# Attention into two mixture layers on one core: maxima of the keys as a tree, the opening in another order, weight splits and routing steps in other places

## The chip, the cores and the metric

The kernel runs on one core of a Trainium2 chip. The metric is the device time of one execution in microseconds (us). Line numbers (L298) are lines of the kernel before.

## The reference

Three stages follow one another, all in fp32. The attention has 8 batches, 8 heads, 576 positions and 64 features; a softmax over the features is taken of the queries and a softmax over the positions of the keys, so that each head needs only a 64x64 product of keys and values.

```python
q_s = exp(q - max(q, -1));  q_s /= sum(q_s, -1) + 1e-9        # over 64 features
k_s = exp(k - max(k, seq)); k_s /= sum(k_s, seq) + 1e-9       # over 576 positions
kv  = einsum('bhsd,bhse->bhde', k_s, v)
x   = einsum('bhsd,bhde->bhse', q_s, kv).transpose(0, 2, 1, 3).reshape(4608, 512)
h   = x @ w_in                                                # 512 -> 2048
x   = (h * clip(h + 3, 0, 6) / 6) @ w_out                     # 2048 -> 512
e   = argmax(x @ w_gate, 1)                                   # one of 8 experts for each token
out = softmax(x @ w_gate)[e] * sigmoid(x @ w_output_gate)[e] * (relu(x @ w1[e]) @ w2[e])
```

The weights `w_in` and `w_out` arrive as 64-bit floats and are turned into fp32 on the chip.

## The kernel before

*Tiling.* The first part (attention, the dense layers and the choice of the expert) goes over 16 groups of 288 tokens (96 partitions by 3), two groups to a batch. A group takes 16 steps, one for each 128 of the 2048 hidden columns (`fb`). A step of group `g` issues, in this order: `h_mm` (L390, the product with `w_in`), `h_ev` (activation on Scalar at L398, product on Vector at L399, from group 1 on a cast on Scalar at L405 and a subtraction on GpSimd at L406), `tail` (the last copies of the group before), the attention work of the *next* group that `att_steps` assigns to this step, `x2_mm` of the step three earlier (L417, the product with `w_out`), and last a routing step of the group *before*: `route1` at step 4, `route2` at 6, `route3` at 9, `route4` at 11. The second part, over the routed tokens, starts when all 16 groups are through.

*Order.* All this is written out by hand. Each engine takes its instructions in the order in which they are written, and an instruction that waits holds up what is behind it on its engine. A step's order in the code is so also the order on TensorE, Scalar, Vector and GpSimd.

*Splits.* Group 0 multiplies in plain fp32 with whole weights. From group 1 on each operand is a sum of two fp32r parts, high and low, and a product is three matmuls for each 128 of the depth: 12 for `h_mm` and 12 for `x2_mm` in a step. `split` makes the two parts of a weight: a cast on Scalar (L200), then a subtraction (L202), on Vector for "in" (`w_in`) and on GpSimd for "out" (`w_out`). It takes a slot of the pool `wsl` (33 slots) for the pair and gives the slot of the raw weight back behind the subtraction. Group 0 decodes the raw weights (`dec_act` on Scalar, `dec_vec` on Vector) and splits "in" 0 at step 5 and "in" 1 and 2 at steps 14 and 15. Group 1 splits at each step the "in" weight that is used three steps later, and the "out" weight of that step.

*Attention.* The keys of a batch are worked on in four head pairs during the odd group before the batch (groups 1, 3, ... 13) and, for the first batch, in the opening. For each pair: `k_max` (maximum over six rows of a partition, L275), `k_max_tr` (transposed on TensorE), `k_max_diag` (maximum over partitions, and a diagonal matrix `dg` of it, L292), `k_max_row` (`kmrow`, L298, which spreads the maximum over all partitions), `k_sub` (L306), `k_exp` (L311), `kv_mm` (L319), and `kv_ev` (L326 to L330, division by the sum, into `kvbd`). For each group: `q_a`, `q_exp`, `q_b`, then `q_tr` (transposed queries `qtps`, copied to `qT` at L363) and `x0_mm` (L376) four times each. The copies of the result to `xhi` (L377) and `xlo` (L379) are what the next group's `h_mm` reads.

*Routing.* `route2` transposes the logits (`ltps`, L460), copies and adds them (L462, L463) and picks the expert. `route3` counts tokens by two small matmuls (`rkps`) and goes on at L490 to L494.

*PSUM.* Eight banks: two for `h_mm` (pool `ph`), four for `x2_mm` (pool `pacc`), and two (pool `pat`) for everything else: `kmps`, `kmrow`, `kvps`, `qtps`, `x0ps`, `lgps`, `ltps` and `rkps` take these in turn.

*Opening.* Before group 0 the first batch's keys and queries are worked on one after the other, and `pe_warm` issues matmuls (L220) whose result nobody reads. `load_k`, `load_q`, `load_v` and `load_w_raw` are issued ahead of all.

Of the kernel before, what the change touches and what calls it, by code (L numbers as in the profile page):

```python
# [8 lines left out]
F32 = mybir.dt.float32  # L9
# [6 lines left out]
ALU = mybir.AluOpType  # L16
AX = mybir.AxisListType
# [3 lines left out]
def kernel(  # L21
# [13 lines left out]
    nc = tc.nc  # L35
    B, H, S, D = q.shape
# [4 lines left out]
    PR = S // R  # L41
# [83 lines left out]
    def big(shape, dt, tag, bufs, name):  # L125
        return sb.tile(shape, dt, tag=tag, name=name, bufs=bufs)
# [145 lines left out]
    def k_max(b, hp):  # L272
        t = kt[b, hp]
        m = sb.tile([PR, 2, D], F32, tag="km", name="km", bufs=2)
        nc.vector.tensor_reduce(out=m, in_=t.rearrange("p r h d -> p h d r"), axis=AX.X, op=ALU.max)  # L275
        kmp[b, hp] = m

    def k_max_tr(b, *hps):
# [62 lines left out]
    def q_exp(g, a):  # L341
        t = qt[g, a].rearrange("p r h d -> p (r h d)")
        nc.scalar.activation(out=t, in_=t, func=ACTF.Exp)
# [520 lines left out]
    with tc.manual_schedule():  # L864
# [17 lines left out]
        pe_warm(10)  # L882
        k_max(0, 0)
        k_max_tr(0, 0)
        q_a(0, 0)
        q_exp(0, 0)
        k_max_diag(0, 0)
        k_max_row(0, 0)
        k_max(0, 1)
        k_max_tr(0, 1)  # L890
        k_sub(0, 0)
        k_exp(0, 0)
        v_pad(0, 0)
        k_max_diag(0, 1)
        k_max_row(0, 1)
        q_b(0, 0)
        k_max(0, 2)
        k_sub(0, 1)
        k_max_tr(0, 2)
        k_exp(0, 1)  # L900
        v_pad(0, 1)
        kv_mm(0, 0)
        k_max_diag(0, 2)
        k_max_row(0, 2)
        kv_ev(0, 0)
        q_a(0, 1)
        k_max(0, 3)
        k_sub(0, 2)
        q_tr(0, 0)
        k_max_tr(0, 3)  # L910
        kv_mm(0, 1)
        k_exp(0, 2)
        v_pad(0, 2)
        q_exp(0, 1)
        k_max_diag(0, 3)
        k_max_row(0, 3)
        kv_ev(0, 1)
        k_sub(0, 3)
        x0_mm(0, 0)
        q_tr(0, 1)  # L920
        k_exp(0, 3)
        v_pad(0, 3)
        kv_mm(0, 2)
        q_b(0, 1)
        dec_act(0)
        x0_mm(0, 1)
        kv_ev(0, 2)
        dec_vec(0)
        kv_mm(0, 3)
        q_tr(0, 2)  # L930
        dec_act(1)
        kv_ev(0, 3)
        dec_vec(1)
        x0_mm(0, 2)
        q_tr(0, 3)
        x0_mm(0, 3)
        dec_act(2)
        dec_act(3)
        for g in range(NG):
            st = att_steps(g + 1)  # L940
            for fb in range(NF):
                h_mm(g, fb)
                if g == 0:
                    load_w_raw(2)
                    decode_step(fb + 1)
                    if fb in (5, NF - 2, NF - 1):
                        split("in", max(0, fb - NF + 3))
                    if fb == 14:
                        gate_weights()
                if g == 0 and fb == 13:  # L950
                    clear_table()
                if g > 0 and fb == 2:
                    logits(g - 1, 0)
                    x2_ev(g - 1, 3)
                h_ev(g, fb)
                if g == 1:
                    if fb + 3 < NF:
                        split("in", fb + 3)
                if g > 0:
                    tail(g - 1, fb)  # L960
                if g == 1:
                    if fb < NF - 1:
                        split("out", fb)
                    if fb == 3:
                        split("out", NF - 1)
                for f in st[fb]:
                    f()
                if fb >= 3:
                    x2_mm(g, fb - 3)
                if fb == NF - 1:  # L970
                    x2_mm(g, fb - 2)
                if g > 0:
                    if fb == 4:
                        route1(g - 1)
                    if fb == 6:
                        route2(g - 1)
                    if fb == 9:
                        route3(g - 1)
                    if fb == 11:
                        route4(g - 1)  # L980
                if g == NG - 2 and fb == 11:
                    plan_first(g - 1)
                if g == NG - 1:
                    if fb == 1:
                        b_tab(0)
                    if fb == 2:
                        b_tab(1)
                    if fb == 3:
                        b_idx(0)
                    if 4 <= fb < 8:  # L990
                        b_gather(0, 2 * fb - 8)
                        b_gather(0, 2 * fb - 7)
                    if fb == 5:
                        for c in range(4):
                            b_load(0, c)
                    if 10 <= fb < 14:
                        b_x(0, fb - 10)
                    if fb >= 7 and fb < 15:
                        for c in (2 * fb - 14, 2 * fb - 13):
                            b_split(0, c)  # L1000
                            if c + 4 < NCH:
                                b_load(0, c + 4)
# [134 lines left out]
```

## Time and profile before

| | us |
|---|---|
| median of 3 runs | 1475.05 (1471.15 to 1476.66) |
| the profiled execution | 1475.42 |
| its span in the profile | 1473.7 |
| TensorE busy in the span | 1405.4 |
| VectorE busy | 868.1 |
| ScalarE busy | 677.7 |
| GpSimd busy | 480.8 |
| opening, before the first matmul of group 0 | 33.87 |
| group 0 | 65.38 |
| group 1 | 84.61 |
| group 2, an even one | 55.61 |
| group 3, an odd one | 64.35 |

The mean granted clock of TensorE over the span is 0.989 of full speed. The times of the groups are distances between the first matmuls of `h_mm` in the trace. In the profile PE is TensorE (matmuls), PEld its weight loads, DVE is VectorE, ACT is ScalarE, POOL is GpSimd. `out<-in` are the program's names for the tiles. A bracket at the end of a row, as in `[0.92 <-DVE w L202]`, says how long the engine stood idle before the instruction and which one ended that.

The views in the section on rows have these columns. *Stretches*: the stretch and its length, then busy time and number of instructions of PE, PEld, DVE, ACT and POOL, then the granted clock of TensorE (1.00 is 2.4 GHz, the upper of two levels, 1.2 GHz is the lower), the busy share of the DMA engines, and GB/s. *Waits*: who waits for whom, then total us, number of waits, the longest. *Timeline*: start and length in us, engine, line, operation, tiles and shapes, number of instructions of one kind in a row. *Groups by line and form*: the number of instructions, their busy time and the mean ns of one, then the idle time of the engine ahead of them.

### The profile page before, as it was taken

What the parts mean: (1) busy time and instruction counts of PE and PEld (TensorE: products, weight loads), DVE (VectorE), ACT (ScalarE), POOL (GpSimd) and SP (SyncE); (2) the same over time, 40 slices, a digit from 0 to 9 for tenths busy, and PEclk for the clock granted to TensorE, in tenths of its full rate; (3) what the DMA queues carried; (4) which work ended last, traced back from release to release, by engine and by line L of the source; (5) the groups of instructions that cost most, each with busy time, mean ns of one, the idle gap of its engine ahead of it and who ended that gap; (6) DMA issues with size and microseconds to landing.
All of it is one profiled execution on the core that took longest, in us unless ns stands there. A gap on an engine that the chain in (4) does not pass through costs nothing. (4 is left out here: it accounts for less than half of the span.)

```text
span 1473.7 us, 27644 instructions
## 1 busy us (share of the span) xinstructions
PE 1405.4 (95%) x9728; PEld 1319.8 (90%) x9728; DVE 868.1 (59%) x2164; ACT 677.7 (46%) x1494; POOL 480.8 (33%) x546
## 2 busy tenths in 40 slices
PE   6997799999999999999999999999999899999997
PEld 5776799999999999999999999999878788888886
DVE  6976454544734635545454473647878476766743
ACT  5855433433433433343343343345555465555642
POOL 1114423222223222222322222245454544445431
PEclk7999999999999999999999999999999999999998
DMA  9912021220221202212122020034767676777773
GB/s 308 306 31 50 17 57 25 49 49 17 58 52 23 49 17 57 48 27 57 25 49 49 18 57 17 2 103 144 239 200 229 187 234 212 246 222 232 232 257 122
DMA packets 195750, 161.19 MB, mean 109 GB/s; under 512 B 116828, under 2 KB 147793, under 8 KB 195602
## 3 DMA queue, kind: packets, MB, share of 16 engines
q1 hardware_dynamic: 186114, 139.51, 32.7%
q0 software_dynamic: 9488, 19.82, 4.3%
q8 instruction: 79, 1.29, 0.4%
q14 instruction: 69, 0.57, 0.1%
HBM read 139.03 MB, written 20.49 MB: 108 GB/s over the span
## 5 line engine op out<-in xcount | busy, mean ns | idle before, releaser
L417 PE MATMUL acc<-gh,w 128*128 128x288 f32 x1920 | 437.6, 305 | 0.0
L390 PE MATMUL hps<-xhi,w 128*128 128x288 f32 x1920 | 425.2, 297 | 0.0
L406 POOL TENSOR_TENSOR gl<-r,gh 128x288 fp32r<-128x288 f32 x240 | 194.2, 811 | 600.0 <-ACT gh L405 556.2
L417 PEld LDWEIGHTS acc<-gh,w 128*128 128x128 f32 x1920 | 321.1, 189 | 3.5
L390 PEld LDWEIGHTS hps<-xhi,w 128*128 128x128 f32 x1920 | 321.4, 188 | 0.9
L399 DVE SCALAR_TENSOR_TENSOR r<-r,hps 128x288 f32<-128x288 f32 x240 | 108.2, 451 | 316.2 <-ACT r L398 308.4
L390 PE MATMUL hps<-xlo,w 128*128 128x288 f32 x960 | 283.2, 295 | 0.0
L417 PE MATMUL acc<-gl,w 128*128 128x288 f32 x960 | 283.0, 295 | 0.0
L398 ACT ACTIVATE r<-hps,half 128x288 f32<-128x288 f32 x240 | 120.1, 500 | 278.6 <-PE hps L390 275.4
L817 PE MATMUL h2ps<-x2h,wb 128*128 128x256 f32 x1088 | 217.3, 282 | 6.4 <-DVE hl L822 4.5
L771 POOL DMA_INDIRECT gx<-x2d,idx x148 | 162.0, 1094 | 145.9 <-issue 132.3
L736 DVE TENSOR_TENSOR wb<-rawb,wb 128x512 fp32r<-128x512 f32 x296 | 191.8, 688 | 14.0 <-ACT wb L735 5.5
L817 PEld LDWEIGHTS h2ps<-x2h,wb 128*128 128x128 f32 x1088 | 176.2, 188 | 16.0 <-DVE hl L822 8.2
L835 PE MATMUL y<-wb,hh 128*128 128x512 f32 x592 | 189.1, 401 | 1.4 <-issue 1.4
L417 PEld LDWEIGHTS acc<-gl,w 128*128 128x128 f32 x960 | 181.7, 189 | 3.0
L390 PEld LDWEIGHTS hps<-xlo,w 128*128 128x128 f32 x960 | 180.9, 188 | 0.2
L405 ACT CAST gh<-r 128x288 fp32r<-128x288 f32 x240 | 103.9, 433 | 152.8 <-DVE r L399 152.3
L735 ACT CAST wb<-rawb 128x512 fp32r<-128x512 f32 x296 | 167.9, 618 | 0.0
L817 PE MATMUL h2ps<-x2l,wb 128*128 128x256 f32 x544 | 152.8, 281 | 3.8 <-DVE x2l L801 3.0
L821 ACT ACTIVATE hh<-h2ps 128x256 fp32r<-128x256 f32 (+1 forms) x160 | 59.0, 369 | 180.3 <-PE h2ps L817 93.4
L822 DVE SCALAR_TENSOR_TENSOR hl<-h2ps,hh 128x256 fp32r<-128x256 f32 (+1 forms) x160 | 63.4, 396 | 126.9 <-ACT hh L821 70.0
L835 PE MATMUL y<-wb,hl 128*128 128x512 f32 x296 | 117.3, 396 | 1.7 <-issue 1.7
(201 smaller groups left out, 1730.6 us busy)
## 6 DMA issues: line engine op xcount, KB each, us to landing
rawb<-in_moe_w_dram SPq DMA_DIRECT2D x296, 256.0 KB
x2d<-xrow SPq DMA_DIRECT2D x60, 144.0 KB
raw<-in_moe_w_in_dram SPq DMA_DIRECT2D x16, 512.0 KB
raw<-in_moe_w_out_dram SPq DMA_DIRECT2D x16, 512.0 KB
qt<-in_q_dram SPq DMA_DIRECT2D x112, 72.0 KB
kt<-in_k_dram SPq DMA_DIRECT2D x56, 144.0 KB
vt<-in_v_dram SPq DMA_DIRECT2D x56, 144.0 KB
w1h<-in_moe_w_dram SPq DMA_DIRECT2D x24, 256.0 KB
```

Of the source, the lines that this page charges most:

```text
L390: nc.tensor.matmul(ps[:, 0:G], weight("in", fb, part, kk), x[:, kk, :], start=(n == 0), stop=(n == len(parts) * KD - 1))
L398: nc.scalar.activation(out=r, in_=ps[:, 0:G], func=ACTF.Relu, bias=half, scale=1.0 / 6.0)
L399: nc.vector.scalar_tensor_tensor(out=r, in0=r, scalar=1.0, in1=ps[:, 0:G], op0=ALU.min, op1=ALU.mult)
L405: nc.scalar.copy(gh, r)
L406: nc.gpsimd.tensor_tensor(out=gl, in0=r, in1=gh.bitcast(F32), op=ALU.subtract)
L417: nc.tensor.matmul(acc[g][eb][:, 0:G], weight("out", fb, part, eb), x, start=(fb == 0 and n == 0), stop=(fb == NF - 1 and n == len(parts) ...
L735: nc.scalar.copy(w[:, 0, :], raw)
L736: nc.vector.tensor_tensor(out=w[:, 1, :], in0=raw, in1=w[:, 0, :].bitcast(F32), op=ALU.subtract)
L771: nc.gpsimd.indirect_dma_start(out=st["gx"][:, kk, :], out_offset=None, in_=x2q, in_offset=bass.IndirectOffsetOnAxis(ap=st["idx"][:, kk:kk ...
L817: nc.tensor.matmul(ps[:, 0:m], w[:, wl, c], x[:, kk, 0:m], start=(kk == 0 and n == 0), stop=(kk == KD - 1 and n == 2))
L822: nc.vector.scalar_tensor_tensor(out=hl[:, 0:m], in0=ps[:, 0:m], scalar=0.0, in1=hh[:, 0:m].bitcast(F32), op0=ALU.max, op1=ALU.subtract)
L835: nc.tensor.matmul(st["y"][t2], hx[:, c], w[:, wl, :], start=(fb == 0 and n == 0), stop=(fb == NF2 - 1 and n == 2))
```

## The change

The maximum over six rows of the keys is taken by three operations of two inputs each (384, 128 and 128 elements for a partition) instead of one reduction; the result of the first is a scratch tile in the slots of `xs`. In the opening the steps of the four head pairs are interleaved otherwise, pairs 2 and 3 share the operations that follow their maxima, `q_a` stands further back, and three more `pe_warm` of 4 matmuls each are written between the steps. Of the "in" splits, 0 to 6 are now made in group 0 (at steps 5 and 12 to 15) instead of 0 to 2; group 1 makes the other nine, seven steps ahead of their use instead of three, and issues both its splits ahead of `h_ev` instead of behind it. `route2` and `route3` are issued behind `h_ev`, ahead of `tail` and of the step's attention work, instead of at the end of the step.

```diff
--- before.py
+++ after.py
@@ -272,7 +272,10 @@
     def k_max(b, hp):
         t = kt[b, hp]
         m = sb.tile([PR, 2, D], F32, tag="km", name="km", bufs=2)
-        nc.vector.tensor_reduce(out=m, in_=t.rearrange("p r h d -> p h d r"), axis=AX.X, op=ALU.max)
+        m3 = big([PR, 3, 2, D], F32, "xs", 3, "km3")
+        nc.vector.tensor_tensor(out=m3, in0=t[:, 0:3], in1=t[:, 3:6], op=ALU.max)
+        nc.vector.tensor_tensor(out=m, in0=m3[:, 0], in1=m3[:, 1], op=ALU.max)
+        nc.vector.tensor_tensor(out=m, in0=m, in1=m3[:, 2], op=ALU.max)
         kmp[b, hp] = m
 
     def k_max_tr(b, *hps):
@@ -882,57 +885,57 @@
         pe_warm(10)
         k_max(0, 0)
         k_max_tr(0, 0)
-        q_a(0, 0)
-        q_exp(0, 0)
+        pe_warm(4)
+        k_max(0, 1)
         k_max_diag(0, 0)
         k_max_row(0, 0)
-        k_max(0, 1)
         k_max_tr(0, 1)
+        pe_warm(4)
         k_sub(0, 0)
         k_exp(0, 0)
         v_pad(0, 0)
         k_max_diag(0, 1)
         k_max_row(0, 1)
-        q_b(0, 0)
-        k_max(0, 2)
+        pe_warm(4)
+        q_a(0, 0)
+        q_exp(0, 0)
         k_sub(0, 1)
-        k_max_tr(0, 2)
         k_exp(0, 1)
         v_pad(0, 1)
         kv_mm(0, 0)
-        k_max_diag(0, 2)
-        k_max_row(0, 2)
+        k_max(0, 2)
+        k_max(0, 3)
+        k_max_tr(0, 2, 3)
+        kv_mm(0, 1)
+        q_b(0, 0)
+        k_max_diag(0, 2, 3)
+        k_max_row(0, 2, 3)
         kv_ev(0, 0)
-        q_a(0, 1)
-        k_max(0, 3)
         k_sub(0, 2)
-        q_tr(0, 0)
-        k_max_tr(0, 3)
-        kv_mm(0, 1)
         k_exp(0, 2)
         v_pad(0, 2)
+        q_tr(0, 0)
+        kv_ev(0, 1)
+        q_a(0, 1)
         q_exp(0, 1)
-        k_max_diag(0, 3)
-        k_max_row(0, 3)
-        kv_ev(0, 1)
         k_sub(0, 3)
-        x0_mm(0, 0)
-        q_tr(0, 1)
         k_exp(0, 3)
         v_pad(0, 3)
         kv_mm(0, 2)
+        x0_mm(0, 0)
+        q_tr(0, 1)
         q_b(0, 1)
+        kv_ev(0, 2)
+        kv_mm(0, 3)
+        x0_mm(0, 1)
         dec_act(0)
-        x0_mm(0, 1)
-        kv_ev(0, 2)
+        q_tr(0, 2)
+        kv_ev(0, 3)
         dec_vec(0)
-        kv_mm(0, 3)
-        q_tr(0, 2)
-        dec_act(1)
-        kv_ev(0, 3)
-        dec_vec(1)
         x0_mm(0, 2)
         q_tr(0, 3)
+        dec_act(1)
+        dec_vec(1)
         x0_mm(0, 3)
         dec_act(2)
         dec_act(3)
@@ -943,8 +946,8 @@
                 if g == 0:
                     load_w_raw(2)
                     decode_step(fb + 1)
-                    if fb in (5, NF - 2, NF - 1):
-                        split("in", max(0, fb - NF + 3))
+                    for f in {5: (0,), 12: (1,), 13: (2,), 14: (3, 4), 15: (5, 6)}.get(fb, ()):
+                        split("in", f)
                     if fb == 14:
                         gate_weights()
                 if g == 0 and fb == 13:
@@ -952,17 +955,20 @@
                 if g > 0 and fb == 2:
                     logits(g - 1, 0)
                     x2_ev(g - 1, 3)
-                h_ev(g, fb)
                 if g == 1:
-                    if fb + 3 < NF:
-                        split("in", fb + 3)
-                if g > 0:
-                    tail(g - 1, fb)
-                if g == 1:
+                    if fb + 7 < NF:
+                        split("in", fb + 7)
                     if fb < NF - 1:
                         split("out", fb)
                     if fb == 3:
                         split("out", NF - 1)
+                h_ev(g, fb)
+                if g > 0 and fb == 6:
+                    route2(g - 1)
+                if g > 0 and fb == 9:
+                    route3(g - 1)
+                if g > 0:
+                    tail(g - 1, fb)
                 for f in st[fb]:
                     f()
                 if fb >= 3:
@@ -972,10 +978,6 @@
                 if g > 0:
                     if fb == 4:
                         route1(g - 1)
-                    if fb == 6:
-                        route2(g - 1)
-                    if fb == 9:
-                        route3(g - 1)
                     if fb == 11:
                         route4(g - 1)
                 if g == NG - 2 and fb == 11:
```

## Rows read from the trace of the kernel before

**Rows 1.** Opening and three groups: busy time of each engine by stretch, with clock, DMA share and GB/s

```profile
0.00:33.87 33.87, 22.25 (x101) 19.11 (x101) 21.95 (x58) 16.60 (x30) 6.37 (x19) 0.70 1.01 302
...
99.25:183.86 84.61, 66.46 (x468) 61.24 (x466) 48.46 (x105) 42.74 (x91) 37.12 (x37) 1.00 0.12 29
183.86:239.47 55.61, 55.61 (x420) 54.79 (x419) 25.84 (x70) 20.72 (x50) 15.72 (x21) 1.00 0.19 44
239.47:303.82 64.35, 62.85 (x475) 61.21 (x474) 36.23 (x92) 25.92 (x62) 15.87 (x21) 1.00 0.16 38
```

**Rows 2.** TensorE's waits in 99.25:183.86: total us, times, longest

```profile
PE kmrow L298 <- DVE dg L292: 3.4, 2, 3.0
...
PE ltps L460 <- ACT kvbd L330: 2.6, 1, 2.6
```

**Rows 3.** timeline of group 1, casts of splits: start, length in us

```profile
102.61 1.21 ACT L200 CAST w<-raw 128x512 fp32r<-128x512 f32 x2
...
123.69 0.65 ACT L200 CAST w<-raw 128x512 fp32r<-128x512 f32 x1 [0.92 <-DVE w L202]
```

**Rows 4.** groups by line and form, VectorE, whole span

```profile
L275 DVE TENSOR_REDUCE km<-kt 96x128 f32<-96x768 f32 x28 | 42.6, 1542 | 0.0
...
L306 DVE TENSOR_TENSOR kt<-kt,kmrow 96x768 f32<-96x768 f32 x28 | 26.4, 944 | 1.6 <-PE kmrow L298 1.6
...
L335 DVE TENSOR_REDUCE qm<-qt 96x12 f32<-96x768 f32 x28 | 26.4, 944 | 0.0
...
L463 DVE TENSOR_TENSOR L<-L,ltps 96x48 f32<-96x48 f32 x16 | 3.2, 199 | 22.2 <-ACT L L462 21.2 <-ACT gh L405 1.0
```

**Rows 5.** timeline of the opening, and one `kv_mm` of group 1

```profile
1.56 4.08 PE L220 MATMUL warm<-ident 128*128 128x128 f32 x20 [1.56 <-POOL ident L94]
...
24.43 2.84 PE L319 MATMUL kvps<-vt,kt 96*128 96x129 f32 x12
...
34.07 0.40 ACT L377 COPY xhi<-x0ps 128x288 f32<-128x288 f32 x1 [0.84 <-PE x0ps L376]
...
125.13 1.61 PE L319 MATMUL kvps<-vt,kt 96*128 96x129 f32 x12 [2.12 <-ACT kt L311]
```

**Rows 6.** timeline of the end of group 0

```profile
95.30 0.50 ACT L398 ACTIVATE g<-hps,half 128x288 f32<-128x288 f32 x1 [2.82 <-PE hps L390]
...
95.84 0.45 DVE L399 SCALAR_TENSOR_TENSOR g<-g,hps 128x288 f32<-128x288 f32 x1 [1.15 <-ACT g L398]
...
96.22 0.46 DVE L379 TENSOR_TENSOR xlo<-x0ps,xhi 128x288 fp32r<-128x288 f32 x1
```

**Rows 7.** timeline of step 6 in odd group 3

```profile
262.04 1.50 PE L319 MATMUL kvps<-vt,kt 96*128 96x129 f32 x12
262.30 0.50 ACT L398 ACTIVATE r<-hps,half 128x288 f32<-128x288 f32 x1 [2.33 <-PE hps L390]
...
263.32 0.43 ACT L405 CAST gh<-r 128x288 fp32r<-128x288 f32 x1 [0.52 <-DVE r L399]
...
265.06 0.33 PE L460 MATMUL ltps<-ident,lt 32*96 32x32 f32 x3
...
265.42 0.20 ACT L462 COPY L<-ltps 96x48 f32<-96x48 f32 x1 [1.13 <-PE ltps L460]
```

**Rows 8.** timeline of steps 9 and 10 in odd group 3

```profile
274.58 0.60 PE L298 MATMUL kmrow<-dg,onesf 128*96 128x256 f32 x2
...
275.13 0.46 DVE L399 SCALAR_TENSOR_TENSOR r<-r,hps 128x288 f32<-128x288 f32 x1 [0.86 <-ACT r L398]
...
275.95 0.39 ACT L363 COPY qT<-qtps 128x288 f32<-128x288 f32 x1
...
278.68 0.16 DVE L490 COPY of<-of 96x8 f32<-96x8 f32 x1
...
279.40 0.17 DVE L494 TENSOR_TENSOR rc<-of,rkps 96x24 f32<-96x24 f32 x1
...
279.72 0.72 PE L376 MATMUL x0ps<-qT,kvbd 128*128 128x288 f32 x2 [1.19 <-DVE rc L494]
```

## The prediction

> **What bounds the kernel now.** I read the busy times by group first, then TensorE's waits, then the timeline at the places where the change puts something. A group of the first part is 288 tokens, and TensorE sets its pace: the even group in [rows 1] is busy for all of its 55.61 us, and an odd group, which also works on the next batch's keys, for 62.85 of 64.35. So whatever another engine does inside a group is free unless TensorE's next instruction waits for it. Three stretches are not at that pace. The opening, before the first expert matmul, takes 33.87 us with TensorE busy for 22.25 and its clock at 0.70 on the mean. Group 0 is full but for its first steps. Group 1 does an odd group's work and takes 84.61 us [rows 1], 20.3 more than the next odd group. The second part, the routed experts, is not touched.
>
> In group 1 TensorE waits for the keys' diagonal, for the exponentials and for a PSUM bank of the `pat` pool [rows 2]. Behind them stands a loop between ScalarE and VectorE: an "in" split casts on Scalar, subtracts on Vector, and gives its raw slot back; the "out" split's cast takes that slot, so it waits 0.92 us for the subtract. At the group's start, with two slots free, the two casts run back to back [rows 3].
>
> **The change part by part.**
>
> Tree of maxima. No row shows it. 768 elements of a two-input operation cost 0.944 us and 48 cost 0.199 [rows 4], so 1.035 ns an element; 384 elements are then 0.55 us, 128 are 0.28, and the three operations with two handovers of 0.04 come to 1.19 us. The reduction costs 1.54 [rows 4]. That is 0.35 us less on Vector, 28 times; the bounds are 0.9 (the slope alone, no fixed cost after the first) and 1.9 us (each operation at twice the slope, which is what the reduction pays against `qm`'s of the same size, nearly). In steady groups Vector is idle for 28 of 64 us [rows 1] and the maxima have steps of slack, so I take nothing for it; if they had none, the two at step 0 would give 0.7 in each of six groups, 4 us in all. The scratch tile shares slots with the `xs` copies, which Scalar writes one step later; Vector is through by then, price 0, at most 0.3 per odd group. A rule speaks against this edit: VectorE: DVE Perf Modes (the Trainium skill, Rules for kernel authors) says to cut the count of chained Vector operations. By its formula for fp32 in the errata section, 151 cycles and one per element at 0.96 GHz, an estimate is 0.96 us for the reduction and 1.14 for the tree, so 5 us more Vector time in all. The trace agrees for `qm`, whose 768 elements take 0.944, and differs for `km`, at 1.54 [rows 4]; the measurement decides, and the sum holds no term from it.
>
> Opening. Moving `q_a(0, 0)` behind two key maxima takes 1.9 us of Vector work (two operations of 0.944) out of the keys' way, and 4 maxima get 0.3 shorter. Against that, the third and fourth maximum and `q_b(0, 0)` now stand ahead of the diagonal for pairs 2 and 3. Following the written order by these prices I get the exponential of pair 2 about 1 us earlier. Behind it Scalar has the same copies to do as before, up to the last `xhi` copy that ended at 34.47 [rows 5]. The 12 added warm-up matmuls (24 passes at 0.2 us, 20 passes having filled the 4.08 us of their first use, about 4.9 us) fall into the 11.6 us in which TensorE stands idle [rows 1]. What they buy is the clock: a `kv_mm` takes 2.84 us here at the lower level and 1.61 in group 1 at the upper one [rows 5]. If it stays up, Scalar's waits for TensorE shrink and the last `xhi` copy ends 2.5 us earlier; if it does not, the third `kv_mm` and `x0_mm` come so late that the gain is lost, and up to 1.1 more. I take 2.0 (nearer to the first, since passes now stand in each gap), bounds 2.5 and -1.1. Group 0 begins behind that copy and Scalar's decoding, and so as much earlier.
>
> Four "in" splits moved from group 1 into the last steps of group 0. There: four casts of 0.65 and four subtracts of about 0.69. Scalar waits 2.82 us for TensorE before the last `h_ev` and Vector 1.15 after it [rows 6], so Vector runs 2.8 - 1.15 = 1.6 late and the last `xlo`, which ended at 96.68, ends at 98.3, ahead of group 1's first matmul at 99.25: price 0, and 0.7 without that cover. In group 1: steps 9 to 12 lose the cast and the wait of the "in" split, 4 x (0.65 + 0.92) = 6.3 us [rows 3], and Scalar's loop sets the pace there. Of that I count 6.0.
>
> Splits ahead of `h_ev` in group 1. Scalar can now cast while TensorE works, but the "in" subtract stands on Vector ahead of `h_ev`'s product, and behind the previous step's attention work; the "out" cast still waits for the subtract, and the activation is behind that cast. The loop of a step keeps its four parts (cast, subtract, cast, then activation, product and second cast), only begins elsewhere. TensorE's longest wait for the diagonal (3.0 us, [rows 2]) gets shorter by about 1.5, but the two new waits below fall on a Vector that is late, and take that back. Price 0; bounds -4.6 (five further waits of 0.92 gone) and +3.
>
> Route steps, the decisive term. `route2` and `route3` move ahead of the step's attention work. `pat` has two PSUM banks for all of attention and routing. At step 6 of an odd group one bank holds `kvps` of pair 0, which `kv_ev` of the same step frees. Before, `kv_mm` of pair 1 took the other and ran at once at 262.04 [rows 7], and the route's `ltps` came after it, with the copy of `L` at 265.42. Now `ltps` takes that other bank, and `kv_mm` must wait until Scalar and Vector are done with it: activation at 262.30, behind it the product, the second cast, which the product releases, from 263.32, then the copy of `L` (0.34 later, an estimate from how closely Scalar's instructions follow one another, and 0.20 long), and the sum with `ltps` (0.20, [rows 4]), which ends at 264.09. A matmul starts 0.15 after the Vector operation that it waits for (0.15 from 279.57 to 279.72, [rows 8]), so at 264.24 instead of right behind the three transposes (0.33, less 0.08 that I take to overlap with the next, an estimate) at 262.29: 1.95 us in which TensorE stands. Were the other bank handed out, it would be later still, since `kv_ev`'s copies are behind the same queue. So 1.95 is a lower bound; the row 2.6 of [rows 2], `ltps` behind `kvbd`, is the same contest in group 1.
>
> At step 9 `rkps` takes a bank ahead of the query transposes and `kmrow`. Banks are handed out in the order in which they came free: `kmrow` started at 274.58, before the copy of the transposes at 275.95 that would free theirs [rows 8]. So `kmrow` now waits for `rkps`, whose last reader is the operation at L494. From L490 to there takes 279.57 - 278.68 = 0.89 us; behind the product (275.13 to 275.59; a next operation starts 0.07 before the end of one, 96.22 against 96.29 in [rows 6]) that ends at 276.41, and `kmrow` starts at 276.56 rather than 274.65, the place that the route's two small matmuls leave it (0.07 behind 274.58, an estimate): 1.9 us. The wait that it replaces, `x0_mm` behind L494, is gone: 1.19. What Vector and Scalar do next comes later by about 2 us, but the same Vector work is left and the pair's `k_sub` still ends ahead of its use at step 11.
>
> An odd group so becomes longer by 1.95 + 1.9 - 1.19 = 2.65 us (2.0 to 3.0). There are six such groups besides group 1 (3 to 13): 15.9 us. In even groups no key work follows: `ltps` waits for nobody, and the query's copy, now behind the small exponential of the route, ends about when `x0_mm` wants it; price 0, at most 0.2 in each of seven.
>
> Sum: -2.0 (opening) - 6.0 (group 1) + 15.9 = +7.9. The profiled execution took 1475.4 us, so 1483.3; it is 0.4 above the median of the runs, and I predict 1483 us.
>
> **The rivals.**
>
> *Group 1 catches up.* If Scalar runs far enough ahead that the nine remaining "in" splits cost no waits, five further waits of 0.92 go (4.6), and the opening gives its 2.5: 15.9 - 10.6 - 2.5 = +2.8, 1478. For it: Scalar waits for TensorE before many activations. Against: Vector's subtract is behind the attention work of the step before. It ends within no change; the point from which it decides is a group 1 below 75 us.
>
> *TensorE's clock falls in group 1.* The wait at step 6 there is longer than 1.95, since product and cast are late: up to 5 or 6 us by the order of the queues. In the opening, with its idle stretches, the clock was at half; at the longest wait in group 1 (3.0 us) it stayed at the upper level [rows 1, 2]. If it falls, one step's matmuls (55.61 over 16 steps, 3.5 us) take twice as long; with the opening's gain gone too, 15.9 - 6 + 3.5 = +13.4, 1489. TensorE: Matmul & The Clock Gate (the Trainium skill, the table of its last part) warns of such idle gaps between bursts; the opening agrees, the waits of up to 3.0 us in group 1 do not show it.
>
> *The banks cost nothing.* If `kv_mm` and `kmrow` found a free bank after all, the moves would only remove the waits for L494: -1.2 x 6 - 2 - 6 = -15, 1460. Against it stands that two banks are two: `kvps` of pair 0 is live at that point.
>
> **How the numbers follow.** Forecast (1480 to 1487) 0.45, first rival 0.27, second 0.18, third 0.10. A measurement can tell about 0.5%, 7.4 us: above 1482.4 lie 0.31 of the forecast and the second rival, 0.49; within, 0.14 and the first rival, 0.41; faster is the third, 0.10. The range goes from 1473 (first rival with both its bounds) to 1491 (second with 3.0 in each odd group); it leaves out the third rival and the tails.
>
> **What would show it.** Odd groups 3 to 13 of about 67.0 us, even ones unchanged at 55.6; in TensorE's waits `kvps` behind L463 (about 2 us) and `kmrow` behind L494 (1.9), seven times each, and none of `x0ps` behind L494; group 1 at 77 to 80 us; the first expert matmul at 31.9; the tree at 1.2 us. Odd groups at 64 or below make the prediction wrong, whatever the rest does; a group 1 below 72 would do so too.

## The result, and the profile after

The changed kernel takes 1493.84 us (median of 4 runs, 1490.55 to 1501.11), against 1474.93 of the kernel before: ratio 1.0136 (95% interval 1.0116 to 1.0156), 18.9 us slower. The forecast was 1483 with a range of 1473 to 1491. The profiled execution has a span of 1492.05 us, 18.4 more than the 1473.65 before. Lines from L276 on stand three further down than before (L298 is now L301).

Where the 18.4 us are, by the distances between the first matmuls of `h_mm`:

| stretch | before | after | measured | forecast |
|---|---|---|---|---|
| opening | 33.87 | 33.23 | -0.6 | -2.0 |
| group 0 | 65.38 | 65.83 | +0.45 | 0 |
| group 1 | 84.61 | 82.82 | -1.8 | -6.0 |
| odd groups 3 to 13, six | 64.34 to 64.37 | 67.80, 66.34, 66.11, 67.98, 66.17, 66.33 | +14.6 | +15.9 |
| even groups 2 to 14, seven | 55.62 (mean) | 56.09 (mean) | +3.3 | 0 |
| from group 15 to the end | 514.3 | 516.8 | +2.5 | 0 |

The view by stretches of the changed kernel (length, busy time of PE, PEld, DVE, ACT, POOL, granted clock, DMA share, GB/s): the opening, group 0, group 1, even group 2, odd groups 3 and 5, as in [rows 1].

```profile
0.00:33.23 33.23, 22.01 (x122) 19.30 (x123) 20.20 (x63) 15.76 (x29) 6.29 (x19) 0.85 1.01 286
33.23:99.06 65.83, 63.31 (x262) 50.15 (x260) 61.51 (x100) 54.41 (x100) 8.67 (x7) 0.97 0.69 217
99.06:181.88 82.82, 70.75 (x468) 67.37 (x466) 44.64 (x108) 39.46 (x85) 36.47 (x37) 0.92 0.13 30
181.88:238.00 56.12, 55.88 (x419) 54.83 (x418) 25.95 (x70) 20.61 (x50) 15.67 (x21) 1.00 0.19 43
238.00:305.80 67.80, 64.24 (x475) 62.73 (x474) 36.59 (x100) 25.99 (x62) 16.18 (x21) 0.97 0.15 36
...
361.90:428.24 66.34, 62.61 (x475) 61.09 (x474) 36.69 (x100) 25.99 (x62) 16.16 (x21) 1.00 0.16 37
```

TensorE has about the same work in an odd group as before (62.6 us busy in group 5, 62.85 in group 3 before), and stands idle for 3.7 us of group 5 where it was 1.5. In groups 1 and 3 the clock is below 1.00, which it was nowhere in these groups before [rows 1].

TensorE's waits over the whole span (total us, times, longest):

```profile
PE kvps L322 <- DVE L L466: 14.7, 7, 4.6
PE kmrow L301 <- DVE rc L497: 12.4, 7, 2.3
PE kmrow L301 <- DVE dg L295: 5.2, 9, 1.7
```

These are the two waits that the prediction named, seven times each, and `x0ps` no longer waits for the count at all. Step 6 of group 3, as in [rows 7]:

```profile
260.57 0.33 PE L463 MATMUL ltps<-ident,lt 32*96 32x32 f32 x3
260.73 0.50 ACT L401 ACTIVATE r<-hps,half 128x288 f32<-128x288 f32 x1 [2.33 <-PE hps L393]
...
261.76 0.43 ACT L408 CAST gh<-r 128x288 fp32r<-128x288 f32 x1 [0.52 <-DVE r L402]
262.09 0.19 ACT L465 COPY L<-ltps 96x48 f32<-96x48 f32 x1
...
262.31 0.20 DVE L466 TENSOR_TENSOR L<-L,ltps 96x48 f32<-96x48 f32 x1 [0.59 <-ACT L L465]
...
262.57 2.90 PE L322 MATMUL kvps<-vt,kt 96*128 96x129 f32 x12 [1.68 <-DVE L L466]
```

The queue is the one that the prediction followed: activation, product, cast, copy, sum, and `kv_mm` behind it, after 1.68 us (1.95 forecast). What the prediction did not have is the length of that `kv_mm`: 2.90 us instead of 1.50 [rows 7]. The stretches of 1 us around it, in group 3 and at the same place of group 5, show why:

```profile
261.00:262.00 1.00, 0.00 (x0) 0.00 (x0) 0.56 (x2) 0.48 (x2) 0.00 (x0) 1.00 0.87 196
262.00:263.00 1.00, 0.43 (x2) 0.43 (x3) 0.62 (x3) 0.28 (x2) 0.73 (x1) 0.82 0.04 10
263.00:264.00 1.00, 1.00 (x7) 1.00 (x7) 0.83 (x6) 0.22 (x1) 0.06 (x1) 0.50 0.00 0
...
385.00:386.00 1.00, 0.00 (x0) 0.00 (x0) 0.62 (x2) 0.48 (x2) 0.00 (x0) 1.00 0.89 190
386.00:387.00 1.00, 0.38 (x3) 0.38 (x4) 0.56 (x3) 0.34 (x2) 0.68 (x1) 1.00 0.00 0
387.00:388.00 1.00, 1.00 (x13) 1.00 (x11) 0.86 (x5) 0.22 (x1) 0.11 (x1) 1.00 0.00 0
```

In group 3 the granted clock goes from 1.00 to 0.50 (from 2.4 to 1.2 GHz) behind the wait and step 6 takes 8.34 us; in group 5 it stays up behind the same wait, and the step takes 6.70. Group 9 is like group 3. The two falls are 3.3 us together.

### The profile page after: what moved, and what is told of

It reads as the page before. It is cut to its first block, busy times and chain, and to the rows that moved or that the text cites. A ratio compares the mean times of both kernels' runs of the same rounds, so it can differ in the third digit from the quotient of the medians.

```text
span 1492.0 us, 27756 instructions
## 1 busy us (share of the span) xinstructions
PE 1418.2 (95%) x9750; PEld 1331.5 (89%) x9750; DVE 870.2 (58%) x2227; ACT 676.4 (45%) x1494; POOL 486.1 (33%) x546
## 5 line engine op out<-in xcount | busy, mean ns | idle before, releaser
L420 PE MATMUL acc<-gh,w 128*128 128x288 f32 x1920 | 442.2, 308 | 0.0
L824 ACT ACTIVATE hh<-h2ps 128x256 fp32r<-128x256 f32 (+1 forms) x160 | 58.8, 368 | 184.5 <-PE h2ps L820 112.8
L825 DVE SCALAR_TENSOR_TENSOR hl<-h2ps,hh 128x256 fp32r<-128x256 f32 (+1 forms) x160 | 63.2, 395 | 129.3 <-issue 68.3
```

The source lines that it names most:

```text
L420: nc.tensor.matmul(acc[g][eb][:, 0:G], weight("out", fb, part, eb), x, start=(fb == 0 and n == 0), stop=(fb == NF - 1 and n == len(parts) ...
L825: nc.vector.scalar_tensor_tensor(out=hl[:, 0:m], in0=ps[:, 0:m], scalar=0.0, in1=hh[:, 0:m].bitcast(F32), op0=ALU.max, op1=ALU.subtract)
```

## The experiments

Each kernel was timed beside the kernel before on the same chip, but not all on one chip, so that ratios can be compared and total microseconds cannot. What can be compared best is the length of the groups. Group lengths in us (clock falls included):

| kernel | group 1 | odd 3 to 13 | even (mean) | ratio |
|---|---|---|---|---|
| before | 84.61 | 64.34 to 64.37 | 55.62 | 1 |
| changed | 82.82 | 66.11 to 66.34, two at 67.8, 67.98 | 56.09 | 1.0136 |
| e1, route steps back | 78.00 | 64.40 to 64.49 | 55.60 | 0.9960 |
| e2, route steps alone | 90.92 | 66.23 to 66.28, two at 67.9 | 56.10 | 1.0165 |
| g2, route2 alone | 89.13 | 66.07 to 66.13, three at 67.6 to 67.7 | 55.64 | one run |
| g3, route3 alone | 87.35 | 64.53 to 64.55, one at 66.11 | 56.09 | one run |
| f3, four splits earlier | 80.71 | 64.32 to 64.37, one at 64.55 | 55.62 | one run |
| f4, splits ahead of `h_ev` | 81.56 | 64.33 to 64.38, one at 64.68 | 55.62 | one run |
| h3, both edits on splits | 76.34 | 64.34 to 64.37 | 55.62 | 0.9951 |

**Which part costs: e1 and e2.** The theory: the two moved route steps. The rival: tree and splits. e1 puts the steps back in the changed kernel, e2 puts them alone into the kernel before.

```diff
-                if g > 0 and fb == 6:
-                    route2(g - 1)
-                if g > 0 and fb == 9:
-                    route3(g - 1)
...
+                    if fb == 6:
+                        route2(g - 1)
+                    if fb == 9:
+                        route3(g - 1)
```

> The changed kernel with the two route steps back at the end of their steps; tree, opening and splits stay. Theory (the route steps are what costs): the waits of kv_mm for the sum of the logits (1.7 us) and of kmrow for the count (1.7 us) are gone, the one of x0_mm for the count (about 1.2) is back; odd groups 64.4 us instead of 66.3, even ones 55.6 instead of 56.1, no fall of the clock in groups 3 and 9; group 1, without the wait of 4.6 us at step 6 and the half clock behind it, 74 to 77 us. Together 1467 to 1471 us. Rival (tree and splits cost, the route steps only show it): odd groups stay at 65 us or above, group 1 above 80, and the time above 1480 us.

> The kernel before with nothing but the two route steps moved ahead of the step's attention work. Theory: everything that the whole change costs is in this: six odd groups at 66.3 us (+2.0), one or two of them 1.7 us longer by a fall of the clock, even groups at 56.1 (+0.45), group 1 longer than before, by 3 to 8 us; 1491 to 1500 us. Rival (other parts cost): odd groups at 64.4, 1475 us.

e1: ratio 0.9960 (0.9948 to 0.9972); e2: 1.0165 (1.0135 to 1.0195). The two moved steps alone cost all of the change (1.0165 is not clear of the 1.0136 of the whole), and the rest gains 0.4%. Odd and even groups came out as expected in both; group 1 fell a little short of it in e1 (78.0, not 74 to 77) and was 6.3 longer in e2. The waits of e1, where the old pair is back and both new ones are gone:

```profile
PE x0ps L379 <- DVE rc L497: 8.7, 7, 1.4
...
PE ltps L463 <- ACT kvbd L333: 2.1, 1, 2.1
```

Group 1 of e1, with the columns of [rows 1], to be held against the changed kernel's above:

```profile
99.14:177.14 78.00, 67.06 (x468) 62.78 (x466) 44.33 (x108) 39.02 (x85) 36.62 (x37) 0.98 0.13 31
```

The route steps make group 1 longer by 4.8 us (78.00 to 82.82). Only 1.1 of it is idle time of TensorE (10.94 to 12.07); 3.7 is busy time for the same matmuls (67.06 to 70.75), at a mean clock of 0.92 instead of 0.98.

**Banks or queues: e3, e4, f1, g1.** That TensorE waits for `L466` shows what it waits for, not why. The bank theory says that the logits' transposes hold one of two `pat` banks; the rival, that Vector and Scalar are late and the keys would wait for them anyway. So the transposes and the counts were given other room: the columns 288 to 511 of the step's own `h_mm` bank.

```diff
+        hb[g] = ps[:, G:]
...
-        p2 = pat.tile([128, 512], F32, tag="a", name="ltps")
+        p2 = hb[g + 1] if g + 1 < NG else pat.tile([128, 512], F32, tag="a", name="ltps")
-        p3 = pat.tile([128, 512], F32, tag="a", name="rkps")
+        p3 = hb[g + 1] if g + 1 < NG else pat.tile([128, 512], F32, tag="a", name="rkps")
```

> The changed kernel, with the logits' transposes and the two counting matmuls put into the unused columns of the step's own h_mm bank instead of a bank of the attention's pool; order of all engines as in the changed kernel. Bank theory: both new waits (kv_mm behind the logits' sum, kmrow behind the count) are gone and x0_mm does not wait for the count either; odd groups 62.6 us, group 1 72 to 76, even groups still 56.1 since their 0.45 comes from Scalar's queue and not from a bank; 1458 to 1464 us. Rival (Vector and Scalar are late because the route's small operations stand ahead of the keys' work): TensorE waits as long as before for something of the keys, odd groups stay at 65 us or above, 1485 us or more.

> The kernel before, with the logits' transposes and the counting matmuls in the unused columns of the step's own h_mm bank; nothing else. Bank theory: the waits of x0_mm for the count (8.5 us in seven) and of the transposes for kvbd in group 1 (2.6 us) go; odd groups 62.9 us, even ones 55.6, group 1 80 to 83; 1460 to 1465 us. Rival (the wait for the count hides another that ends no sooner): odd groups at 64 us or above, 1473 to 1475 us.

e3 missed: ratio 1.0142 (1.0114 to 1.0171), odd groups 65.2 to 65.4, even ones 58.1. Both waits behind the route steps were gone, but the edit had brought two of its own (e3, TensorE's waits):

```profile
PE hps L466 <- DVE r L405: 20.0, 15, 4.0
PE hps L493 <- DVE r L405: 18.7, 15, 2.8
```

The transposes now stood behind the product of `h_ev`, which reads another part of the same bank. PSUM — Partial Sum Buffer (the Trainium skill, section on bank collisions) says to guard PSUM by bank and not by address; the program is guarded so, the wait is there although the columns differ, and what would happen without it no run shows. e4 changed nothing (0.9999, 0.9985 to 1.0014): the wait of `x0ps` for the count was gone, and in an odd group 0.82 us for `xlo` at the query transposes (9.9 in eight over the span, 2.9 in two before) and 0.43 for the activation at `kv_mm` stood in place of 1.19, so odd groups stayed at 64.35 to 64.37, but for one of 65.86 in which the clock fell. There the rival was right.

In f1 the changed kernel's transposes and counts go into that bank right behind `h_mm`, ahead of the reads.

```diff
+                if g > 0 and fb == 6:
+                    pre2(g - 1)
+                if g > 0 and fb == 9:
+                    pre3(g - 1)
                 h_ev(g, fb)
```

> The changed kernel, with the logits' transposes and the counting matmuls in the unused columns of the step's own h_mm bank and issued right behind h_mm, ahead of h_ev's reads of that bank. In the run with them behind h_ev they waited 1.14 us for the product that reads the same tile (and more in group 1), which hid what the attention's two banks are worth; here nothing stands in their way. Bank theory: TensorE waits neither for the logits' sum nor for the count nor at the transposes; odd groups 62.6 to 63.2 us (65.2 less two waits of 1.14), even ones 56.1, group 1 72 to 76 and its clock up at step 6; ratio to before 0.985 to 0.993. Rival (Vector and Scalar late): other waits of the same length for the keys' work take their place, odd groups at 65 or above, ratio 1.005 or more.

Ratio 0.9985 (0.9970 to 1.0000), odd groups 64.02 to 64.05 (one 64.35). All of the cost in odd groups is gone by giving the matmuls another bank, with the order on TensorE, Scalar and Vector as in the changed kernel: so it was the banks. The size was missed: the expected 62.6 to 63.2 were too low by 1 us, group 1 took 78.36 and not 72 to 76, and the ratio lies above the expected 0.985 to 0.993. The waits of f1 show what came next:

```profile
PE qtps L364 <- DVE xlo L382: 4.1, 8, 1.1
PE kvps L322 <- ACT r L404: 3.3, 6, 0.5
```

Even groups stayed at 56.15: their 0.47 us are not a matter of banks. g1 adds e1's order to f1's banks:

> The changed kernel with the route steps back at the end of their steps, and only their matmuls (logits' transposes, counts) put ahead, right behind h_mm and into the unused columns of its bank. Theory (two causes: the attention's banks are taken, and Scalar's and Vector's queue is): both are away, so even groups are back at 55.6 us, odd ones at 64.0 or a little less (as with the early matmuls alone, where the wait for xlo at the query transposes takes over), group 1 75 to 78; ratio to before 0.991 to 0.995. Rival (as in the kernel before with the matmuls late in the h_mm bank): odd groups stay at 64.4, ratio 0.996 or above.

Ratio 0.9966 (0.9951 to 0.9981): even groups 55.57, odd ones 64.33 to 64.38 but for 64.81 and, with a fall of the clock, 65.87, as the rival had it; group 1 took 80.70, where 75 to 78 was expected. Giving the routes their own room is worth nothing where they stand behind the attention work.

**One route step at a time: g2, g3.**

> The kernel before with only route2 moved ahead of the attention work of step 6. By the prediction's step: kv_mm waits 1.7 to 1.95 us for the logits' sum in each odd group, nothing else changes: odd groups 66.2 us (67.9 where the clock falls behind that wait), even groups 55.6, group 1 longer by the wait of about 4.9 less the 2.6 that the transposes waited, 86 to 91 us. Rival (route2 and route3 are only bad together): odd groups at 65 or below.

> The kernel before with only route3 moved ahead of the attention work of step 9. By the prediction's step: kmrow waits 1.7 to 1.9 us for the count in odd groups and x0_mm no more: odd groups 64.6 to 65.1 us. From the changed kernel's steps 9 to 12 (1.96 longer, then 1.51 and 0.25 shorter): 64.6. Even groups 56.1, all of what they lost (their query copy is behind the route's last small exponential on Scalar). Rival (the even groups' 0.45 comes from route2 or the tree): even groups 55.6.

Both as expected, with g3's odd groups at the lower end. `route2` costs 1.75 us in an odd group, and falls of the clock behind it. `route3` costs 0.19: `kmrow`'s new wait for the count (13.5 us in seven) takes the place of `x0_mm`'s and of more. Of the even groups' 0.47, all is `route3`'s. The changed kernel at step 9 of group 2 shows how; the exponential stands on Scalar ahead of the queries' copy and waits for Vector's chain:

```profile
216.25 0.20 ACT L508 ACTIVATE rso<-rso 96x3 f32<-96x3 f32 x1 [1.73 <-DVE rso L507]
216.36 0.38 ACT L366 COPY qT<-qtps 128x288 f32<-128x288 f32 x1
...
216.78 0.75 PE L379 MATMUL x0ps<-qT,kvbd 128*128 128x288 f32 x2 [0.24 <-ACT qT L366]
```

**Why the clock falls: f2, h1, h2.** In f2 five matmuls that nobody reads follow the transposes and the counts of odd groups of the changed kernel; h1 does so in g2 (behind the transposes alone), h2 in e2.

```diff
             nc.tensor.transpose(p2v[:, r, :], lt[:, r * PR:(r + 1) * PR], ident[0:32, 0:32])
+        warm_into(p2, 5 if g % 2 == 0 else 0)
...
+    def warm_into(ps, n):
+        for _ in range(n):
+            nc.tensor.matmul(ps[:, 256:384], ident, ident, start=True, stop=True)
```

> The changed kernel with five matmuls that nobody reads (128x128 each) behind the logits' transposes and behind the counting matmuls in odd groups: TensorE works through most of each wait of 1.7 us and the following matmuls start when they did. Theory (the clock falls because TensorE stands still): no odd group of 67.9 us, all of 3 to 13 at 66.2 to 66.6; group 1, whose wait of 4.6 us is only partly filled, still shows a fall; mean clock 0.987 or higher; ratio 1.009 to 1.013. Rival (the falls come from something else): one to three odd groups still at 67.9 or more, ratio 1.0136 or above.

> The kernel before with route2 moved, and five matmuls that nobody reads behind the logits' transposes in odd groups. Without them three of the six odd groups were at 67.7 us and three at 66.1. Theory (the clock falls because TensorE stands still for 1.7 us): all six at 66.1 to 66.3, none at 67.6 or more, and no half clock at step 6; group 1 (wait of 4.9 only partly filled) may still fall. Rival (the falls come by themselves and no fall in the first filled run was luck): two or three of six at 67.6 or more.

> The kernel before with both route steps moved, and the same five matmuls in both waits of odd groups. Without them two of the six odd groups were at 67.9 us. Theory: all six at 66.2 to 66.6, even ones at 56.1. Rival: one to three at 67.8 or more.

Odd groups: 66.33 to 66.57 in f2, 66.22 to 66.30 in h1, 66.44 to 66.50 in h2, none of 18 with a fall. Without the filling, 7 of 18 had one at step 6 (2 in the changed kernel, 2 in e2, 3 in g2). f2's ratio is 1.0130 (1.0099 to 1.0161), so the gain is not clear of the changed kernel's 1.0136 in the time itself. Step 6 of group 3 in f2, to be held against the rows of the changed kernel above; the wait that is left is 0.52 us and the clock stays up:

```profile
260.02 0.32 PE L467 MATMUL ltps<-ident,lt 32*96 32x32 f32 x3
260.28 1.38 PE L454 MATMUL ltps<-ident 128*128 128x128 f32 x10
...
262.18 1.05 PE L322 MATMUL kvps<-vt,kt 96*128 96x129 f32 x7 [0.52 <-DVE L L471]
```

```profile
261.00:262.00 1.00, 0.66 (x6) 0.47 (x5) 0.26 (x2) 0.63 (x2) 0.28 (x1) 1.00 0.42 94
262.00:263.00 1.00, 0.82 (x7) 0.82 (x8) 0.83 (x5) 0.21 (x1) 0.51 (x1) 1.00 0.00 0
```

So at step 6 it is the standing still that lets the clock fall. Why only in some groups with the same wait, stays open, and the length of the wait alone does not say: behind `kmrow`'s wait of 1.68 to 1.69 us at step 9 it fell in 1 of 18 groups (in g3, none in the changed kernel and e2), and in one group each of e4 and g1 it fell at step 11 behind two short waits, of 0.8 and some 0.5 us, with the route steps in their old place.

**The edits on splits: f3, f4, h3.** Each alone in the kernel before, then both.

```diff
-                    if fb in (5, NF - 2, NF - 1):
-                        split("in", max(0, fb - NF + 3))
+                    for f in {5: (0,), 12: (1,), 13: (2,), 14: (3, 4), 15: (5, 6)}.get(fb, ()):
+                        split("in", f)
...
-                    if fb + 3 < NF:
-                        split("in", fb + 3)
+                    if fb + 7 < NF:
+                        split("in", fb + 7)
```

> The kernel before with only the four 'in' splits moved from group 1 to the end of group 0 (seven steps ahead instead of three); both splits of a step stay behind h_ev. As predicted: group 0 as long as before (65.4 us), group 1 shorter by 6.0: 78.6. Rival (what TensorE waits for in group 1 is the attention's banks and not the splits): 82 to 84 us.

> The kernel before with only the place of the splits in a step of group 1 changed (ahead of h_ev instead of behind it), three steps ahead as before. As predicted: group 1 at 84.6 us, no change (between 80 and 87.6). Rival (Scalar casts while TensorE works, so five waits of 0.92 for the subtraction go): 80 us; other rival (h_ev is late behind the casts and x2_mm waits for it): 87 us or more.

> The kernel before with both edits on the splits (four more in group 0, and ahead of h_ev in group 1), without the tree, the opening's order and the moves of the route steps. Alone the edits shortened group 1 by 3.9 and 3.05 us. If they add up: group 1 at 77.7, ratio to before 0.995 to 0.996, the same as with tree and opening (0.996), which so are worth nothing. Rival (tree and opening carry part of the gain of that run): ratio 0.998 or above.

Group 1: 80.71 with the four splits moved (-3.9), 81.56 with the other order (-3.05), 76.34 with both (-8.3), more than the two together. So the forecast was wrong on both: f3 lies between its theory (78.6) and its rival, and f4 is not without effect. h3 has the lowest ratio of the study, 0.9951 (0.9933 to 0.9968), as good as e1 without tree and opening. These two are worth nothing that can be measured. TensorE's clock takes part here too: its mean in group 1 is 1.00 in f3 and 0.96 in f4 and h3. Group 0 stayed at 65.36 to 65.42 in f3 and h3: the cover in its last steps held.

**The opening: g4.** In the opening of the changed kernel:

```profile
15.74 1.79 PE L322 MATMUL kvps<-vt,kt 96*128 96x129 f32 x12
...
17.02 1.47 POOL L355 TENSOR_TENSOR qt<-qt,qs 96x768 f32<-96x768 f32 x1 [13.77 <-DVE qs L353]
...
17.12 1.66 DVE L295 TENSOR_SCALAR dg<-ident,mc 128x128 f32<-128x128 f32 x2
...
22.75 2.92 PE L322 MATMUL kvps<-vt,kt 96*128 96x129 f32 x12 [2.21 <-ACT vt L252]
...
33.83 0.37 ACT L380 COPY xhi<-x0ps 128x288 f32<-128x288 f32 x1
```

Two diagonal operations that take 0.29 each elsewhere take 1.66 here, while GpSimd multiplies (the first 1.50, which ends 0.13 behind GpSimd's operation, the second 0.27). The clock was up for `kv_mm` of pairs 0 and 1 (1.52 and 1.79 us, 2.86 and 2.84 before); `kv_mm` of pair 2, behind a wait of 2.21 us, runs at the lower clock as before [rows 5]. The last `xhi` copy ends at 34.20, 0.27 earlier than before. In g4, on top of e1:

```diff
-        q_b(0, 0)
         k_max_diag(0, 2, 3)
         k_max_row(0, 2, 3)
+        q_b(0, 0)
```

> The changed kernel with the route steps back, and in the opening q_b(0, 0) behind the diagonal of pairs 2 and 3 instead of ahead of it. Theory (the two diagonal operations took 1.66 us instead of 0.58 because they ran beside GpSimd's product of q_b): they take 0.6 us, kmrow of pairs 2 and 3 comes 1 us earlier, and what follows up to the first matmul of group 0 as much as 1 us earlier (32.3 instead of 33.3). Rival (the two diagonal operations are slow by themselves when they are a pair): 1.6 us as before. Other rival (the end of the opening hangs on another chain): they take 0.6, and the first matmul of group 0 stays within 0.3 of 33.3.

The pair of diagonals (g4):

```profile
15.98 0.48 DVE L295 TENSOR_SCALAR dg<-ident,mc 128x128 f32<-128x128 f32 x2
...
33.14 0.40 ACT L380 COPY xhi<-x0ps 128x288 f32<-128x288 f32 x1
```

They take 0.48 us, and the last `xhi` copy ends 0.66 earlier than in the changed kernel's profile (34.20 to 33.54); group 0's first matmul was at 32.90 instead of e1's 33.33, between theory and rival. It is one run, and openings differ by more between runs: group 1 began at 98.8 to 101.5 us in the six kernels with the changed opening, and at 96.6 to 99.3 in the ten with the old one. So no gain of the changed order shows: the first matmul of group 0 came at 33.0 to 36.1 us in those six and at 31.2 to 34.0 in those ten.

## Why the prediction was wrong

*What held.* In the odd groups, the mechanism and its place. The two new waits are there, seven times each; the wait of `x0ps` for the count is gone; an undisturbed odd group is 1.9 us longer (four of 66.11 to 66.34 less 64.35), a little under the 2.0 to 3.0 forecast: `kv_mm` waits 1.68 (1.95 forecast), `kmrow` 1.7 (12.4 less group 1's 2.3, over six; 1.9 forecast), and more than the counted 1.19 went away at steps 10 and 11 (1.5 and 0.25). f1 shows that it is the banks, as argued. That the six odd groups cost 14.6 us against 15.9 is luck: the moved steps themselves cost 11.3, and two falls of the clock, which the forecast did not have there, add 3.3.

*What failed.* The main step is what TensorE's clock does behind the new waits. The sum held nothing for it, since the clock had stayed up behind the 3.0 us wait of [rows 2]; it cost 3.7 us in group 1 (of 4.3 that the clock took there in all) and 3.3 in groups 3 and 9. Next is the price 0 of the even groups.

1. Group 1, 4.2 us. The forecast took 6.0 off and let the two new waits there be "taken back" by a shorter wait for the diagonal, price 0; a longer wait with a fall of the clock was a rival at 0.18. The waits came out as summed: TensorE stood idle for 12.07 us of group 1 instead of 18.15, 6.1 less (82.82 less 70.75 in the stretches above, 84.61 less 66.46 in [rows 1]). But the same 468 matmul instructions kept it busy for 70.75 us instead of 66.46, at a mean clock of 0.92 instead of 1.00: 4.3 us, all of the miss. In group 1 the rival is what happened, with a price (3.5) near the measured one. By e1, 3.7 of the 4.3 come with the route steps, with a wait of 4.59 us at step 6 where e1's transposes wait 2.1; the other 0.6 is there without them. The sum of the edits on the splits (-6.6 in e1, -6.0 forecast) was right by luck: moving four splits gave 3.9 and not 6.0, and the order 3.05 and not 0.
2. The even groups, 3.3 us. The step "price 0, at most 0.2 in each of seven" named the right operation, the small exponential ahead of the queries' copy, and sized it at less than half: 0.47 each, seven times. What looked like a copy that "ends about when `x0_mm` wants it" ended 0.24 late; where the other 0.2 come from, no row shows.
3. The clock in the steady groups, 3.3 us. The text looked for a fall only in group 1, since the waits of 3.0 us in [rows 2] had kept the clock. One wait of a trace that keeps it does not say that another will: behind the same 1.68 us it fell in 7 of 18 groups. TensorE: Matmul & The Clock Gate (the Trainium skill, the table of its last part) warns of idle gaps between bursts, and the prediction cited it for group 1 alone. The Trainium skill speaks there of longer gaps than these, so the measurement decides: f2, h1 and h2 show that a wait of 1.68 us matters already.
4. The opening and group 0, 1.8 us. The prediction had two branches, the clock stays up (2.5 us gained) or the third `kv_mm` comes so late that the gain is lost, and took 2.0. The mean clock rose (0.85 for 0.70), but not for the third `kv_mm`, and the second branch came: the last `xhi` copy ended 0.27 earlier, and group 0 began 0.6 earlier. The order also put GpSimd's product beside the diagonal, which the text had not followed; what that is worth, one run of g4 does not settle. Group 0's 0.45 goes with the clock: it fell at 40.8 us, behind a wait of 2.41. The four kernels with the changed opening in which it fell at that place (the changed one, e1, e3, g1) have a group 0 of 65.8 to 65.9 us, the other three (f1, f2, g4) one of 65.3.
5. The end, 2.5 us. Group 15, where the two route steps are moved as well, takes 58.8 us up to its last `x2_mm` in both kernels. The 2.5 are in the second part behind it (455.55 to 457.99 us), whose code is the same, with TensorE busy 4.0 us longer at a mean clock of 0.98 instead of 0.99. Nothing shows that the change causes this: that part took 431.5 us in e1 and 439.6 in e4, on one chip.

The profiled span grew by 18.4 us and the sum of the prediction was 7.9: 10.5 missing, of which 4.2 are item 1, 3.3 item 2, 1.8 item 4 and 2.5 item 5, less the 1.3 by which the odd groups were forecast too long (without the falls of item 3 these would have been 11.3, 4.6 below the forecast).

*The tree.* Three operations of 0.56, 0.29 and 0.29 in the opening take 1.21 us with their handovers, 1.19 were forecast. Over the span they are dearer (groups by line and form, VectorE, changed kernel):

```profile
L278 DVE TENSOR_TENSOR km<-km,km 96x128 f32<-96x128 f32 x32 | 19.1, 596 | 1.1
L276 DVE TENSOR_TENSOR km<-kt 96x384 f32<-96x384 f32 x28 | 15.8, 563 | 0.0
L277 DVE TENSOR_TENSOR km<-km 96x128 f32<-96x128 f32 x32 | 10.7, 334 | 1.1
```

The sum of the means is 1.49 us against the reduction's 1.54 [rows 4]: the last operation takes 0.78 where GpSimd's subtraction runs beside it, as in step 5 of group 3 (timeline, changed kernel):

```profile
257.69 0.29 DVE L277 TENSOR_TENSOR km<-km 96x128 f32<-96x128 f32 x1
257.73 0.91 POOL L409 TENSOR_TENSOR gl<-r,gh 128x288 fp32r<-128x288 f32 x1 [2.36 <-ACT gh L408]
258.01 0.78 DVE L278 TENSOR_TENSOR km<-km,km 96x128 f32<-96x128 f32 x1
```

The term 0 was right.

## What to carry to other kernels

Where a few banks serve many short-lived tiles in turn, the place of a small step is the place where it takes a bank: before moving it ahead, list who takes the next bank on the busy engine and when the last reader of the small tile is through. A move that removes a wait has to be followed to the wait behind it (e4 took 8.5 us of waits for the count away and gained nothing). And a wait on TensorE is to be priced with a chance of the clock's fall behind it, in every group in which it stands and not just in the longest.

## What the runs showed of the hardware

Behind a wait of 1.68 us at step 6 the granted clock fell from 1.00 to 0.50 in 7 of 18 groups, and in none of 18 where a wait of about 0.5 us was left; behind one of the same length at step 9 it fell in 1 of 18. Each fall cost some 1.6 us. Vector's maximum of 128 columns takes 0.29 us alone and 0.78 beside a GpSimd operation of 0.91, and a pair of diagonals 1.66 instead of 0.48. SBUF — State Buffer (the Trainium skill, its terms table) describes a port pair that Vector and GpSimd take in turn, each for a whole instruction; the pair of diagonals, 1.66 beside a GpSimd operation of 1.47 us and 0.48 without, agrees with it.
